# Feed-forward weight loads in twelve spaced parts, and an attention output matrix that is zeroed by VectorE and loaded early

## The chip, the cores and the metric

The kernel runs on one core of a Trainium2 chip (trn2). Its time is the device time of one launch in microseconds (us), the slowest core counting; here there is only one. Each execution also records the mean clock granted to TensorE (1.000 is full speed). "Fast" is an execution that is not over 1.5% above the fastest of the same kernel; only fast runs are compared. The engines are PE (TensorE, matrix products), PEld (its weight loads), DVE (VectorE), ACT (ScalarE), POOL (GpSimd) and SP (SyncE, which only issues DMA transfers here).

## The reference, cut to what matters

A transformer block: 2,048 tokens of width 512, 32 heads of width 16, a gated feed-forward layer of width 1,792, and a layer norm before each half whose shift, scale and gate come from a small conditioning vector.

```python
mod = (_silu(c) @ w_mod)            # sa, ca, ga, sb, cb, gb
h = _layernorm(x) * (1 + ca) + sa
q, k, v = split(h @ wqkv)           # 32 heads of 16
p = softmax(q @ k.T * 16 ** -0.5)
x = x + ga * ((p @ v) @ wo)
h = _layernorm(x) * (1 + cb) + sb
x = x + gb * (gelu(h @ w_gate) * (h @ w_up) @ w_down)
```

The costly part is the softmax: 32 x 2,048 x 2,048 exponentials.

## The kernel before: what the change touches

While it is built, the kernel plans its own instruction order. A recorder keeps a cost model of every engine; a loop (`stream`) places score products, exponentials and probability-times-value products, and slips side work (projections, output projection, feed-forward layer) into free TensorE time. What it decides is then fixed: each engine executes its list in order and waits on semaphores. So any change to the recorded operations can also change the order of everything after it.

Most exponentials are ScalarE instructions (`E<-ps_sc`) of three or two 512-column banks. About one bank in thirteen (156 of 2,048) is computed by VectorE in five steps (`dt`, `du`, `du`, `dt`, `ED`) to relieve ScalarE.

The step that finishes the conditioning vector (`modB`) frees the space in which the feed-forward weights are to lie. Everything that waited for that was put right behind it:

```python
    def side_mod(self):
        ...
        self.copy("dve", self.modB[:, :], mi[:, 0:8])
        self.ts("dve", self.modB[:, 4:8], self.modB[:, 4:8], 1.0, None, ALU.add)
        sp, pool = "sp", "pool"
        self.memset(pool, self.wo[:, :, :], 0.0, [self.modB[:, :]])     # after modB
        self.memset(pool, self.self32[:, :], 0.0)
        ...
        self.dma(sp, self.wg[:, :, :], ..., "wg")       # 1,792 KB each
        self.dma(sp, self.wu[:, :, :], ..., "wu")
        self.dma(sp, self.wd[:, :, :], ..., "wd")
        for j in range(4):
            for ee in range(2):                          # 8 loads of 64 KB
                src = self.A_wo.rearrange(...)[j, ee]
                self.dma(sp, self.wo[32 * j:32 * j + DH, ee:8:2, :], src, "wo%d" % (2 * j + ee))
```

`wo` is stored with 16 of every 32 partitions zero, hence the memset.

The same SyncE list carries the small transfers of the softmax denominators. After the last product of a group of four heads, VectorE copies the sums out (`osb`), and four kinds of transfers follow: `scr_den<-osb`, `den<-scr_den`, then after a reciprocal `scr_rec<-rden` and `rb<-scr_rec`. VectorE then forms `onorm = osb * rb`, at a fixed place in its list:

```python
        def fin1():
            self.recip(rden, den)
            self.dma("sp", s2..., rden, "dc%d" % sem)                    # scr_rec<-rden
            for j in range(4):
                self.dma("sp", self.rb[32 * j:32 * j + 32, lo:hi], ...)  # rb<-scr_rec
        def fin2():
            self.tt("dve", self.onorm[:, qd, c:c + W], osb, rb, ALU.mult)
```

The softmax here doesn't subtract the row's maximum and nothing guards it: scores larger than these inputs give would overflow.

## Time and profile before

| | before |
|---|---|
| time, median of three runs | 927.5 us (926.55 to 1,074.73; the longest is slow) |
| span of the profiled run | 925.9 us, clock 0.994 |
| ScalarE busy | 891.0 us, 96% |
| TensorE, VectorE busy | 809.4 us, 767.7 us |
| ScalarE idle from 79 to 125 us | 46.00 - 41.30 = 4.70 us |

The page's span, its busy line, and its chain of waits that ended last (shares of the span, by engine):

```profile
span 925.9 us, 17469 instructions
...
PE 809.4 (87%) x7328; PEld 259.3 (28%) x7328; DVE 767.7 (83%) x1483; ACT 891.0 (96%) x749; POOL 7.7 (1%) x13
...
ACT 82%; PE 8%; DVE 6%; DMA 3%; issue 1%; SPq 0%; DVEq 0%
```

ScalarE is the engine to read. The table by stretches shows where it is not full. Columns: the stretch in us, its length, then for each engine the busy time and the number of instructions, the granted TensorE clock, the DMA share and GB/s.

```profile
core 0: us, PE busy (x) PEld busy (x) DVE busy (x) ACT busy (x) POOL busy (x), PEclk, DMA share, GB/s
46.00:79.00 33.00, 30.48 (x264) 11.35 (x261) 15.93 (x28) 33.00 (x31) 0.00 (x0) 1.00 0.01 2
79.00:125.00 46.00, 38.45 (x315) 12.06 (x312) 39.95 (x67) 41.30 (x34) 4.41 (x3) 0.93 0.51 151
...
231.00:400.00 169.00, 147.39 (x1029) 38.50 (x1025) 154.22 (x285) 168.25 (x140) 0.00 (x0) 1.00 0.05 11
400.00:600.00 200.00, 173.00 (x1227) 46.11 (x1224) 180.48 (x332) 198.87 (x165) 0.00 (x0) 1.00 0.05 14
```

From 79 to 125 us ScalarE is busy 41.30 of 46 us, and the clock averages 0.93. The timeline of ScalarE in the stretch shows the gaps (start, time from there, instruction, count, and in brackets the idle time before it and what ended it):

```profile
88.52 7.52 ACT L309 ACTIVATE E<-ps_sc 128x1536 bf16<-128x1536 f32 x6 [1.35 <-PE ps_sc L296]
96.27 16.29 ACT L309 ACTIVATE E<-ps_sc 128x1536 bf16<-128x1536 f32 x13 [0.22 <-PE ps_sc L296]
113.80 2.54 ACT L309 ACTIVATE E<-ps_sc 128x1024 bf16<-128x1024 f32 x2 [1.25 <-PE ps_sc L296]
116.94 2.96 ACT L309 ACTIVATE E<-ps_sc 128x1536 bf16<-128x1536 f32 x2 [0.60 <-PE ps_sc L296]
120.48 3.77 ACT L309 ACTIVATE E<-ps_sc 128x1024 bf16<-128x1024 f32 x3 [0.58 <-PE ps_sc L296]
124.71 10.91 ACT L309 ACTIVATE E<-ps_sc 128x1024 bf16<-128x1024 f32 x9 [0.46 <-PE ps_sc L296]
```

What runs on Pool when the hole begins, from its timeline:

```profile
81.76 3.51 POOL L337 MEMSET wo<- 128x4096 bf16 x1 [77.46 <-DVE modB L321]
```

And what VectorE's `dt<-dt` takes beside it and just after, from VectorE's timeline:

```profile
81.77 3.77 DVE L321 TENSOR_SCALAR dt<-dt 128x512 f32<-128x512 int32 x1
...
88.56 0.41 DVE L321 TENSOR_SCALAR dt<-dt 128x512 f32<-128x512 int32 x1
```

The second is the same instruction at its usual length, 0.41 against 3.77 us. And SyncE's list, from its timeline, where the time is that spent issuing:

```profile
83.82 0.42 SPq L359 DMA_DIRECT2D mreg<-in_B_w_gate_dram  x1
84.29 0.51 SPq L359 DMA_DIRECT2D mreg<-in_B_w_up_dram  x1
84.84 0.51 SPq L359 DMA_DIRECT2D dreg<-in_B_w_down_dram  x1
85.39 12.25 SPq L359 DMA_DIRECT2D wo<-in_A_wo_dram  x8
97.68 0.42 SPq L359 DMA_DIRECT2D scr_rec<-rden  x1
105.74 1.71 SPq L359 DMA_DIRECT2D rb<-scr_rec  x4
```

The eight `wo` issues hold SyncE for 12.25 us. The view of the tile `wo` gives the shortest, the median and the longest issue in ns:

```profile
L359 SPq DMA_DIRECT2D wo<-in_A_wo_dram x8: 426/426/8970, 85.4 to 97.2; - x8
```

So the first one, right behind the three weight loads, is held for 8.97 us, and each of the other seven takes 0.43 us. In the chain of waits, between 70 and 130 us, the next small transfer follows:

```profile
97.68 8.04 DMA scr_rec<-rden
...
109.14 0.69 DVE onorm L313
```

It takes 8.04 us, and VectorE can form `onorm` only at 109.14 us, after 1.5 us of waiting. What VectorE has in its list behind `onorm` is late with it: TensorE waits 2.11 us until VectorE has made `kmo` (keys for the score products), ScalarE 1.25 us for scores. The record of the clock in this trace shows TensorE at half rate for 6.83 us from 113.5 us on, right behind TensorE's wait, and the gaps of 0.60 and 0.58 us lie in that.

### The profile page before, as it was taken

Reading aid. Unit: us, or ns where it says so; the run is one execution under the profiler, and the core shown is the slowest. Engines: PE = TensorE matmul, PEld = TensorE weight load, DVE = VectorE, ACT = ScalarE, POOL = GpSimd, SP = SyncE. Lnnn points to the kernel's source line nnn. Section 1 sums busy time; section 2 is a strip of 40 time slices with the busy share of each in tenths; the row PEclk is TensorE's granted clock in tenths of the full one; section 3 lists DMA queues with packets and bytes.
Section 4 is the critical chain, followed back from the end, with each engine's and each line's share of the span. In section 5 each row is a group of like instructions: output and inputs, shape, how many; then the busy total and the mean of one; then the engine's idle time right before and its main releaser. Section 6 shows DMA issues by size and latency. Waiting matters only on the chain.

```text
span 925.9 us, 17469 instructions
## 1 busy us (share of the span) xinstructions
PE 809.4 (87%) x7328; PEld 259.3 (28%) x7328; DVE 767.7 (83%) x1483; ACT 891.0 (96%) x749; POOL 7.7 (1%) x13
## 2 busy tenths in 40 slices
PE   8898888878889888888888888888898899988988
PEld 3332222222222222222222222222222223334346
DVE  8748889998997999998897999998998674577864
ACT  6999999999999999999999999999999999999992
POOL 1001000000000000000000000000000000000000
PEclk9999999999999999999999999999999999999999
DMA  9003500000000000000000000000010000000000
GB/s 296 1 1 135 154 13 12 13 13 13 14 13 7 8 12 14 13 13 20 13 18 12 14 13 13 13 1 19 25 26 9 13 8 19 25 14 13 21 8 13
DMA packets 30784, 24.96 MB, mean 27 GB/s; under 512 B 15705, under 2 KB 25490, under 8 KB 30706
## 3 DMA queue, kind: packets, MB, share of 16 engines
q1 hardware_dynamic: 28322, 22.28, 8.5%
q10 hardware_dynamic: 2384, 1.57, 0.6%
q8 instruction: 57, 0.93, 0.4%
q14 instruction: 21, 0.17, 0.1%
HBM read 21.23 MB, written 2.61 MB: 26 GB/s over the span
## 4 chain that ended last, share of the span: by engine, by line
ACT 82%; PE 8%; DVE 6%; DMA 3%; issue 1%; SPq 0%; DVEq 0%
ACT E L309 79%; PE ps_mi L296 4%; PE ps_sc L296 3%; ACT wreg L309 2%; DMA scr_rec<-rden 1%; DVE dt L321 1%; DMA mreg<-in_w_mod_dram 1%; DMA rb<-scr_rec 1%; PE ps_pv L296 1%; DVE du L326 1%; DVE wreg L326 1%; DVE ED L326 1%; DVE wreg L330 1%; SPq L359 0%; DVE onorm L313 0%
## 5 line engine op out<-in xcount | busy, mean ns | idle before, releaser
L309 ACT ACTIVATE E<-ps_sc 128x1536 bf16<-128x1536 f32 (+2 forms) x700 | 864.4, 1467 | 18.2 <-PE ps_sc L296 17.9
L296 PE MATMUL ps_pv<-E,vaug 128*17 128x512 bf16 (+2 forms) x2439 | 184.1, 330 | 3.6 <-ACT E L309 1.4
L296 PE MATMUL ps_sc<-qT,kme 32*128 32x512 bf16 (+2 forms) x1344 | 155.0, 331 | 26.0 <-ACT E L309 20.7
L296 PE MATMUL ps_sc<-qT,kmo 32*128 32x512 bf16 (+2 forms) x1344 | 156.4, 333 | 22.1 <-ACT E L309 17.3
L321 DVE TENSOR_SCALAR dt<-ps_sc 128x512 int32<-128x512 f32 x156 | 107.6, 690 | 41.8 <-PE ps_sc L296 37.8
L296 PE MATMUL ps_mi<-wreg,mreg 128*128 128x512 bf16 (+1 forms) x448 | 122.8, 358 | 12.2 <-DVE wreg L330 5.9
L296 PE MATMUL ps_sc<-xs,ident 128*128 128x512 bf16 x283 | 92.7, 386 | 35.8 <-ACT E L309 32.9
L326 DVE SCALAR_TENSOR_TENSOR ED<-du,dt 128x512 int16<-128x512 f32 x156 | 106.3, 684 | 0.7
L326 DVE SCALAR_TENSOR_TENSOR du<-du,dt 128x512 f32<-128x512 f32 x156 | 105.4, 681 | 0.5
L326 DVE SCALAR_TENSOR_TENSOR du<-dt 128x512 f32<-128x512 uint16 x156 | 105.3, 684 | 0.3
L296 PEld LDWEIGHTS ps_sc<-qT,kme 32*128 32x128 bf16 x1344 | 41.0, 91 | 140.6 <-ACT E L309 92.6
L296 PEld LDWEIGHTS ps_sc<-qT,kmo 32*128 32x128 bf16 x1344 | 41.5, 91 | 135.3 <-ACT E L309 90.8
L296 PEld LDWEIGHTS ps_pv<-E,vaug 128*17 128x17 bf16 x2439 | 48.1, 88 | 105.8 <-issue 94.4
L321 DVE TENSOR_SCALAR dt<-dt 128x512 f32<-128x512 int32 x156 | 67.8, 439 | 0.6
L296 PE MATMUL ps_mi<-dreg,hreg 128*128 128x512 bf16 x210 | 65.1, 385 | 0.5 <-DVE xw L313 0.2
L296 PE MATMUL ps_pv<-ED,vaug 128*17 128x512 bf16 (+2 forms) x185 | 59.2, 351 | 1.2 <-DVE ED L326 1.2
L296 PEld LDWEIGHTS ps_mi<-wreg,mreg 128*128 128x128 bf16 x448 | 34.9, 97 | 76.8 <-issue 37.1
L330 DVE CAST wreg<-ps_mi 128x512 bf16<-128x512 f32 x49 | 33.7, 688 | 22.9 <-PE ps_mi L296 22.4
L296 PEld LDWEIGHTS ps_sc<-xs,ident 128*128 128x128 bf16 x283 | 20.1, 97 | 85.9 <-ACT E L309 82.8
L296 PE MATMUL ps_mi<-hreg,wreg 128*128 128x512 bf16 x120 | 40.0, 390 | 1.9 <-DVE qT L321 1.1
L326 DVE SCALAR_TENSOR_TENSOR wreg<-wreg,ps_mi 128x512 bf16<-128x512 bf16 x49 | 33.5, 684 | 8.3 <-PE ps_mi L296 7.5
L296 PE MATMUL ps_mi<-wo,onorm 128*128 128x512 bf16 x120 | 38.2, 385 | 1.4 <-DVE xw L313 1.3
(118 smaller groups left out, 510.1 us busy)
## 6 DMA issues: line engine op xcount, KB each, us to landing
rb<-scr_rec SPq DMA_DIRECT2D x96, 64.0 KB, 2.0
mreg<-in_w_mod_dram SPq DMA_DIRECT2D x1, 2048.0 KB, 14.4
out_dram<-xs SPq DMA_DIRECT2D x16, 128.0 KB, 1.7
mreg<-in_B_w_gate_dram SPq DMA_DIRECT2D x1, 1792.0 KB, 7.1
mreg<-in_B_w_up_dram SPq DMA_DIRECT2D x1, 1792.0 KB, 11.2
dreg<-in_B_w_down_dram SPq DMA_DIRECT2D x1, 1792.0 KB, 16.5
rb<-scr_rec SPq DMA_DIRECT2D x56, 32.0 KB, 1.8
wreg<-in_A_wqkv_dram SPq DMA_DIRECT2D x3, 384.0 KB, 10.6
```

Source lines behind the costliest of these rows:

```text
L296: return self.rec("pe", lambda e: e.matmul(out, lhsT, rhs, start=start, stop=stop, tile_position=tp), [lhsT, rhs], [out], cost=(n, int(rhs ...
L309: return self.rec("act", lambda e: e.activation(out, in_, func, scale=scale, **kw), rd, wr, cost=self.cost("act", out, [in_], "act"))
L321: return self.rec(eng, lambda e: e.tensor_scalar(out, a, s1, s2, **kw), rd, [out], cost=self.cost(eng, out, [a], "ts"))
L326: return self.rec("dve", lambda e: e.scalar_tensor_tensor(out, a, s, b, op0=op0, op1=op1), rd, [out], cost=self.cost("dve", out, [a, b], " ...
L330: return self.rec(eng, lambda e: e.tensor_copy(out, in_), [in_], [out], cost=self.cost(eng, out, [in_], "ts"))
```

## The change

The intent: no burst of 5.4 MB ahead of the small transfers, and no long Pool memset while VectorE computes exponentials. The zeros of `wo` become eight VectorE memsets, done with the `wo` loads some 30 us earlier. The feed-forward weights are loaded in twelve parts, eight score banks apart.

```diff
     def side_mod(self):
         ...
-        self.memset(pool, self.wo[:, :, :], 0.0, [self.modB[:, :]])
-        self.memset(pool, self.self32[:, :], 0.0)
+        self.done("modB")
+        yield END
+
+    def side_wo_load(self):
+        if not self.dry:
+            self.task([lambda qd=qd: self.memset("dve", self.wo[:, qd, :], 0.0) for qd in range(8)]
+                      + [lambda: self.memset("dve", self.self32[:, :], 0.0)], "wo0")
+        yield from self.until("wo0")
         ...                                  # affine_select on Pool, as before
-        self.dma(sp, self.wg[:, :, :], ..., "wg")        # and wu, wd: whole
         ...                                  # the eight wo loads, as before
+
+    def weight_parts(self):                  # 4 of wg, 4 of wu, 4 of wd
+        ...
     def plan(self, ends, nsplit):
         w = [(self.side_first, 0, at(30))]
+        w.append((self.side_wo_load, at(30), at(30)))
     def stream(self):
+        parts = self.weight_parts()
         while rp < len(rounds):
+            while parts and "modB" in self.have and pos >= loaded:
+                parts.pop(0)()
+                loaded = pos + 8
```

More of the change, by code (lines that the diff above doesn't have):

```diff
@@ L765, in side_mod @@
         self.ts("dve", self.modB[:, 4:8], self.modB[:, 4:8], 1.0, None, ALU.add)
-        sp, pool = "sp", "pool"
-        self.memset(pool, self.wo[:, :, :], 0.0, [self.modB[:, :]])
-        self.memset(pool, self.self32[:, :], 0.0)
+        self.done("modB")
[5 more added lines that the diff above has]
+        yield from self.until("wo0")
         selv = self.self32[:, :].rearrange("p (a b) -> p a b", b=32)
         self.affine_select(selv, [[-32, 4], [0, 32]], ALU.not_equal, 1.0, -16, 1)
-        self.dma(sp, self.wg[:, :, :], self.B_w_gate.rearrange("(a p) n -> p a n", p=P), "wg")
-        self.dma(sp, self.wu[:, :, :], self.B_w_up.rearrange("(a p) n -> p a n", p=P), "wu")
-        self.dma(sp, self.wd[:, :, :], self.B_w_down.rearrange("(f p) n -> p f n", p=P), "wd")
         for j in range(4):
@@ L776, in side_mod, with part @@
                 src = self.A_wo.rearrange("(a j e r) n -> j e r a n", j=4, e=2, r=DH)[j, ee]
-                self.dma(sp, self.wo[32 * j:32 * j + DH, ee:8:2, :], src, "wo%d" % (2 * j + ee))
+                self.dma("sp", self.wo[32 * j:32 * j + DH, ee:8:2, :], src, "wo%d" % (2 * j + ee))
         yield END
+    def weight_parts(self):
+        def part(dst, src, sem):
+            return lambda: self.dma("sp", dst, src, sem)
+        parts = []
+        for name, t, w in (("wg", self.wg, self.B_w_gate), ("wu", self.wu, self.B_w_up)):
+            v = w.rearrange("(a p) n -> p a n", p=P)
+            parts += [part(t[:, a, :], v[:, a, :], "%s%d" % (name, a)) for a in range(NDC)]
+        v = self.B_w_down.rearrange("(f p) n -> p f n", p=P)
+        parts += [part(self.wd[:, f:f + 4, :], v[:, f:f + 4, :], "wd%d" % f) for f in range(0, 12, 4)]
+        parts.append(part(self.wd[:, 12:NFC, :], v[:, 12:NFC, :], "wd12"))
+        return parts
     def ln2_steps(self, k, src=None):
@@ L1055, in stream @@
         active = []
-        pos = c = e = nd = rp = 0
+        pos = c = e = nd = rp = loaded = 0
         virt = 0.0
```

## The prediction

> **What bounds it.** ScalarE: busy 891.0 of 925.9 us (96%) on the page, and the chain that ended last runs 79% over its Exp instructions. So from 20 to 900 us time is saved only where ScalarE stands idle, or by giving it fewer columns. The stage table shows it full from 23 to 79 us, losing time between 79 and 125 us, full again to about 845 us; its other idle time lies in the first 20 us and the tail, which the diff leaves alone.
>
> **The hole at 79 to 125 us.** ScalarE's timeline has six gaps there: 1.35, 0.22, 1.25, 0.60, 0.58, 0.46 us, together 4.46 us. Two causes, both edited by the diff:
> 1. Pool's memset of wo runs at 81.76 for 3.51 us. Meanwhile one VectorE TENSOR_SCALAR dt<-dt takes 3.77 us (usually 0.42): 3.35 us of VectorE lost. The Trainium skill ("SBUF — State Buffer", "Who interferes with whom") says a VectorE two-port mode and GpSimd exclude each other for a whole instruction; this trace agrees. The 1.35 us gap follows.
> 2. Three 1,792 KB loads and eight wo loads are issued at 83.8 to 97.6 us, the wo issues alone holding SyncE for 12.25 us (1.5 us each; rb issues take 0.43). The next scr_rec gets out only at 97.68 and lands 8.04 us later (chain); rb lands at 109.0. VectorE waits 1.50 us for it in order, TensorE then 2.11 us for kmo, ScalarE 1.25 us. TensorE's thin stretch at 110 to 113 halves its granted clock (0.50 from 114 to 120 us), which makes the gaps of 0.60 and 0.58. "TensorE: Matmul & The Clock Gate" (Part 1) describes that gate; its half rate agrees.
>
> **The change.** Removed: the Pool memset and the burst of 5.4 MB. Added on VectorE: eight 128x256-word memsets, 0.27 us each by the equal-sized dreg memset at 0.92 us, and a small one: about 2.4 us, in the 46 to 69 us stretch where VectorE is busy 9.3 of 23 us: free. It delays side projections by 2.4 us; ScalarE is full there, so they have slack. wo loads start near 50 us on an empty queue. Each of twelve parts is 448 KB (last: 256): at the trace's 350 to 430 GB/s an estimated 1.1 to 1.3 us, some 3 us apart, so a small transfer waits about 1 us instead of 8.
>
> The built order also differs: 154 VectorE exponentials for 156, hence two Exp of 1,536 columns more and two of 1,024 fewer, at ScalarE spacings of 1.34 and 0.91 us: +0.9 us. The two are lost near the onset of VectorE exponentials, about 80 us.
>
> **Sum.** 927.5 - 4.5 (perhaps 0.5 stays) + 0.9 = about 924. Later stages are reshuffled but equally ScalarE-bound: within 1 us or so. VectorE time won back buys nothing more, as the recorded order is fixed.
>
> **What will show it.** On Pool one 0.5 us select near 50 us in place of the burst; no dt<-dt above 0.5 us near 82; scr_rec landing in 2 to 4 us; no half-clock stretch at 113 to 120; ScalarE idle below 1 us from 79 to 125; ScalarE busy 1 us up.
>
> **What would make it wrong.** A new half-clock stretch elsewhere, or the later onset of VectorE exponentials; then no gain. If the rest runs denser than I think, 920 or less. Beyond 2% either way is out of reach: the idle time there is 4.5 us.
>
> Predicted 924.0 us, range 921.0 to 927.3; faster by over 2% 0.01, within 2% 0.98, slower 0.01.

## The result, and the profile after

The changed kernel takes 922.4 us (median of four fast runs, 921.53 to 923.05) against 927.02 us (four runs, with the slow one). The ratio of the fast runs is 0.9956, with a 95% interval of 0.9936 to 0.9976. Ratios here and below are the mean time of one kernel's fast runs over that of the other's of the same rounds, so not quite the ratio of the medians quoted. That is 0.4%. Another chip gave 0.9961 (e7 below).

The page's span, busy line and chain:

```profile
span 919.5 us, 17368 instructions
...
PE 779.0 (85%) x7222; PEld 259.7 (28%) x7342; DVE 759.8 (83%) x1482; ACT 890.8 (97%) x749; POOL 3.6 (0%) x11
...
ACT 89%; PE 6%; DVE 3%; issue 0%; DMA 0%; DVEq 0%
```

(PE's line isn't compared: the page after lists 120 fewer products than weight loads, the page before none.) The table by stretches, columns as before:

```profile
46.00:79.00 33.00, 29.31 (x256) 11.55 (x260) 16.75 (x35) 32.83 (x30) 0.31 (x1) 1.00 0.11 26
79.00:125.00 46.00, 38.84 (x364) 13.35 (x363) 41.97 (x75) 46.00 (x40) 0.00 (x0) 1.00 0.40 133
...
231.00:400.00 169.00, 142.05 (x1015) 38.20 (x1030) 151.51 (x279) 168.77 (x140) 0.00 (x0) 1.00 0.04 11
400.00:600.00 200.00, 168.33 (x1208) 45.85 (x1227) 180.05 (x334) 199.34 (x165) 0.00 (x0) 1.00 0.05 15
```

ScalarE is full from 79 to 125 us, the clock is 1.00 there, and the two losses between 231 and 600 us have shrunk from 0.75 + 1.13 to 0.23 + 0.66 us. ScalarE's timeline from 70 to 140 us has one gap left:

```profile
76.95 64.53 ACT L309 ACTIVATE E<-ps_sc 128x1536 bf16<-128x1536 f32 x53 [0.17 <-PE ps_sc L296]
```

On Pool one short operation is left after 5 us, by its timeline:

```profile
54.15 0.31 POOL L340 TENSOR_SCALAR_AFFINE_SELECT self<-self 128x128 f32<-128x128 f32 x1 [49.86 <-DVE self L337]
```

`dt<-dt` has its usual length, two of them in 0.76 us, by VectorE's timeline:

```profile
84.44 0.76 DVE L321 TENSOR_SCALAR dt<-dt 128x512 f32<-128x512 int32 x2
```

SyncE's list, from its timeline:

```profile
53.62 3.62 SPq L359 DMA_DIRECT2D wo<-in_A_wo_dram  x8
...
80.97 0.35 SPq L359 DMA_DIRECT2D mreg<-in_B_w_gate_dram  x1
83.41 0.33 SPq L359 DMA_DIRECT2D scr_rec<-rden  x1
84.82 1.72 SPq L359 DMA_DIRECT2D rb<-scr_rec  x4
86.58 1.37 SPq L359 DMA_DIRECT2D mreg<-in_B_w_gate_dram  x3
88.00 0.94 SPq L359 DMA_DIRECT2D mreg<-in_B_w_up_dram  x2
```

The `wo` loads take 3.62 us to issue into an empty queue. `scr_rec` is issued at 83.41 and lands 1.4 us later, as the first `rb` goes out at 84.82. But the parts are not evenly spaced on the chip: parts two to six leave together, within 2.4 us from 86.58 us on, since SyncE works in order and had waited for `scr_rec` to land. From 92 to 94 us the DMA still moves 384 GB/s.

The profiled pair differs by more than the medians, 925.9 - 919.5 = 6.4 us. Part of that is luck: the profile before has a second stretch at half clock, near 900 us, which the profile after has not. Such stretches come and go between runs (see "What the Trainium skill lacked").

### The profile page after: what moved, and what is told of

It reads as the page before. It is cut to its first block, busy times and chain, and to the rows that moved or that the text cites. A ratio compares the mean times of both kernels' runs of the same rounds, so it can differ in the third digit from the quotient of the medians.

```text
span 919.5 us, 17368 instructions
## 1 busy us (share of the span) xinstructions
PE 779.0 (85%) x7222; PEld 259.7 (28%) x7342; DVE 759.8 (83%) x1482; ACT 890.8 (97%) x749; POOL 3.6 (0%) x11
## 4 chain that ended last, share of the span: by engine, by line
ACT 89%; PE 6%; DVE 3%; issue 0%; DMA 0%; DVEq 0%
ACT E L309 87%; PE ps_sc L296 3%; PE ps_mi L296 2%; ACT wreg L309 2%; PE ps_pv L296 1%; DVE du L326 0%; DVE st L349 0%; DMA xs<-in_A_x_dram 0%; DVE xw L313 0%; DVE nwt L313 0%; DVE dt L321 0%; ACT hreg L309 0%; DVE hreg L321 0%; DVE wreg L326 0%; ACT L309 0%
## 5 line engine op out<-in xcount | busy, mean ns | idle before, releaser
L309 ACT ACTIVATE E<-ps_sc 128x1536 bf16<-128x1536 f32 (+2 forms) x700 | 865.2, 1489 | 12.9 <-PE ps_sc L296 12.9
L296 PE MATMUL ps_pv<-E,vaug 128*17 128x512 bf16 (+2 forms) x2439 | 180.1, 329 | 3.3 <-DVE vaug L330 1.1
L296 PE MATMUL ps_sc<-qT,kmo 32*128 32x512 bf16 (+2 forms) x1344 | 154.1, 331 | 31.1 <-ACT E L309 26.4
L296 PE MATMUL ps_sc<-xs,ident 128*128 128x512 bf16 x264 | 85.7, 384 | 47.0 <-ACT E L309 45.1
L296 PE MATMUL ps_mi<-wreg,mreg 128*128 128x512 bf16 (+1 forms) x421 | 113.9, 355 | 11.8 <-DVE wreg L326 4.5
L321 DVE TENSOR_SCALAR dt<-dt 128x512 f32<-128x512 int32 x154 | 63.8, 417 | 0.5
L296 PE MATMUL ps_mi<-dreg,hreg 128*128 128x512 bf16 x185 | 56.5, 384 | 2.4 <-issue 1.3
L296 PE MATMUL ps_mi<-hreg,wreg 128*128 128x512 bf16 x105 | 34.0, 385 | 2.5 <-DVE qT L321 0.9
L313 DVE TENSOR_TENSOR wreg<-wreg 128x1024 bf16<-128x1024 bf16 (+1 forms) x56 | 34.7, 619 | 0.5
```

The source lines that it names most:

```text
L296: return self.rec("pe", lambda e: e.matmul(out, lhsT, rhs, start=start, stop=stop, tile_position=tp), [lhsT, rhs], [out], cost=(n, int(rhs ...
L309: return self.rec("act", lambda e: e.activation(out, in_, func, scale=scale, **kw), rd, wr, cost=self.cost("act", out, [in_], "act"))
L313: return self.rec(eng, lambda e: e.tensor_tensor(out, a, b, op), [a, b], [out], cost=self.cost(eng, out, [a, b], "tt"))
L321: return self.rec(eng, lambda e: e.tensor_scalar(out, a, s1, s2, **kw), rd, [out], cost=self.cost(eng, out, [a], "ts"))
```

## The experiments

Comparing the two kernels alone can't tell the causes apart, since the planner gave them different orders. So most experiments keep the order of the kernel before. The recorder got a mode in which an operation is recorded, with its waits, but not seen by the cost model, and a "ghost" that enters the cost of an operation which is not there. The rivals A to D are other explanations; each is stated in the expectation of the run that tests it. Checked instruction by instruction: TensorE's and ScalarE's lists in e1 to e5 and e8 are those of the kernel before, and VectorE's differ by the nine memsets alone.

```diff
     def model(self, op, t, cost):
+        if self.quiet:
+            op.t1 = 0.0
+            return
+    def ghost(self, eng, t, cost, dma=False):
+        ...
+        op = _Op(eng, "d_ghost" if dma else eng, 0, None)
+        self.model(op, max(t, self.free[eng]), cost)
+        return op.t1
```

All experiments compute the right result. Each has five rounds beside the kernel before, on one chip per call (e1 to e4, e5 to e8, e9 to e12); medians are of fast runs. As TensorE, ScalarE and VectorE do the same work in the same order, the time from the 51st to the 101st exponential instruction of ScalarE in the trace measures the hole by itself. It is in the last column, for one profiled execution of each. (Line numbers in the profiles of the experiments are shifted by the added code: L325 is the ScalarE helper that was L309.)

| run | zeros | wo loads | weights | median, us (before) | ratio, 95% interval | 51st to 101st Exp, us |
|---|---|---|---|---|---|---|
| before | Pool, 82 us | after weights | whole | | | 65.56 |
| e1 | VectorE, early | after weights | whole | 928.62 (927.95) | 1.0017 (0.9999 to 1.0036) | 65.64 |
| e2 | Pool, 82 us | before weights | parts | 924.57 (927.95) | 0.9967 (0.9951 to 0.9984) | |
| e3 | VectorE, early, and a Pool memset at 82 us | early | parts | 924.51 (927.95) | 0.9982 (0.9955 to 1.0008) | 61.37 |
| e4 | VectorE, early | early | parts | 924.09 (927.95) | 0.9970 (0.9949 to 0.9991) | 61.03 |
| e5 | VectorE, early | early | whole | 923.35 (927.18) | 0.9959 (0.9944 to 0.9974) | 59.89 |
| e8 | Pool, early | early | parts | 923.57 (927.18) | 0.9974 (0.9951 to 0.9997) | 59.89 |

### e1: only the zeros moved

```diff
-        self.memset(pool, self.wo[:, :, :], 0.0, [self.modB[:, :]])
+        wz = self.ghost(pool, at, 8 * D * 3.0 + 100)     # the plan still sees it
+    def zero(self):                                      # recorded quietly at at(30)
+        for qd in range(8):
+            self.memset("dve", self.wo[:, qd, :], 0.0)
```

> Every instruction of TensorE, ScalarE and VectorE is issued in the order of the kernel before; only the zeros of wo move, from one Pool memset after modB to eight VectorE memsets near 50 us. The three whole weight loads and the eight wo loads stay where they were. Theory (two separate causes, the exclusion of VectorE by the Pool memset worth the gaps of 1.35 and 0.22 us): 1.2 to 1.8 us faster than before, no dt<-dt above 0.5 us near 82 us, scr_rec still landing after about 8 us and the half-clock stretch near 113 us still there. Rival A (absorption: VectorE waits 1.5 us for rb later in any case, so the delay costs nothing in the end): within 0.5 us of before. Rival B (the whole gain is the new instruction order that the planner made): no gain.

No gain at all, where I expected 1.2 to 1.8 us. The long `dt<-dt` and the gap at 87 us are gone, but one gap takes the place of the others. ScalarE's timeline:

```profile
116.36 2.54 ACT L325 ACTIVATE E<-ps_sc 128x1024 bf16<-128x1024 f32 x2 [4.78 <-PE ps_sc L312]
```

SyncE's timeline:

```profile
86.29 12.52 SPq L375 DMA_DIRECT2D wo<-in_A_wo_dram  x8
98.85 0.42 SPq L375 DMA_DIRECT2D scr_rec<-rden  x1
107.75 1.71 SPq L375 DMA_DIRECT2D rb<-scr_rec  x4
```

VectorE, freed earlier, reaches `onorm` earlier and waits there: 4.5 us at one time in the list of waits of that stretch, against 1.5 us before. `scr_rec` still takes 8.9 us. The end of the hole is set by the transfer, so the 3.35 us that VectorE lost to the Pool memset were hidden in front of it. Rival A holds here; the theory of two separate costs falls.

### e2: only the loads in parts

```diff
-        self.dma(sp, self.wg[:, :, :], ..., "wg")        # and wu, wd
+        self.ghost(sp, t, P * 3584 * 4, True)            # one for each; parts quietly in stream
```

> Instruction order of the kernel before on all compute engines; the three loads are issued as twelve spaced parts; the Pool memset of wo and the eight wo loads stay after modB. Theory: the second cause goes and the first stays: scr_rec lands in under 4 us, rb before 95 us instead of 109, no half-clock stretch near 113 us, ScalarE's gaps between 100 and 125 us gone and the 1.35 us gap at 87 us kept: 2.5 to 3.3 us faster than before. Rival B (order): no gain. Rival C (it is the wo loads, waiting on the memset and holding SyncE, and not the size of the burst): gap near 110 us stays, gain under 1 us.

The gain is 3.4 us by the medians, about as expected. `scr_rec` lands in 3.5 us (issued at 90.54, the first `rb` at 94.06). The eight `wo` loads, still at the old place but with an empty queue in front of them, are issued in 3.62 us instead of 12.25. What remains of the hole (0.67, 0.51 and 0.22 us) is partly a half-clock stretch at 83 us that this run happened to have. Its last column is left out for that.

### e3 and e4: all but the exclusion, and all

```diff
 # e3 is e4 with this in the place of the old memset:
+        self.quietly(lambda: self.memset(pool, self.onorm[:, 1:8, :], 0.0, [self.modB[:, :]]))
```

> Instruction order of the kernel before; zeros and wo loads early, loads in twelve parts, and a Pool memset of 128x3584 elements of onorm that nobody needs is put where the memset of wo was. Only the exclusion of VectorE is left of the two causes: the memset takes about 3.1 us, one VectorE dt<-dt takes about 3.3 us near 82 us. Theory: 1.0 to 1.6 us slower than e4_all_order_kept, with a ScalarE gap of about 1 us at 87 us. Rival A (absorbed): as fast as e4_all_order_kept within 0.5 us.

> All three parts of the change, but every instruction of TensorE, ScalarE and VectorE in the order of the kernel before (156 VectorE exponentials instead of 154). Theory: ScalarE idle between 79 and 125 us under 0.5 us, no half-clock stretch near 113 us, 4 to 5.5 us faster than before, and up to 1 us faster than the changed kernel, which gives ScalarE 0.9 us more of columns. Rival B (the gain comes from the new order): within 1 us of before. If it is slower than the changed kernel by over 1 us, the planner's new order is worth something of its own.

The medians, 924.51 and 924.09 us, do not separate the two; both scatter with the clock (0.985 to 1.000). The traces do. In e3 the useless memset runs at 82.64 us for 3.08 us, and the instruction beside it, from VectorE's timeline, is

```profile
82.65 3.35 DVE L337 TENSOR_SCALAR dt<-dt 128x512 f32<-128x512 int32 x1
```

ScalarE's timeline of e3:

```profile
88.88 7.52 ACT L325 ACTIVATE E<-ps_sc 128x1536 bf16<-128x1536 f32 x6 [0.83 <-PE ps_sc L312]
96.62 55.04 ACT L325 ACTIVATE E<-ps_sc 128x1536 bf16<-128x1536 f32 x45 [0.22 <-PE ps_sc L312]
```

The gain of e4 over before, 3.9 us by the medians, is just under the 4 us expected, and rival B (order) falls, since e4 has the old order. In e3 the two gaps of the first cause are there, 0.83 and 0.22 us, where e5 and e8 have none. By the last column the exclusion costs 61.37 - 59.89 = 1.48 us once the transfer is out of the way. The two runs of e3 at clock 0.999 and 1.000 have a span of 921.7 us each, the one of e4 at 1.000 has 920.6: 1.1 us. (The profiled run of e4 had a half-clock stretch of 3.41 us at 83 us, hence its 61.03.) So the predicted price of the memset, 1.35 + 0.22 us, was about right, but it is paid only after the other cause is gone.

### e5 and e6: whole loads again, the rest of the change kept

e5 has the order before, e6 the planner's own.

```diff
 # e5: wo and its zeros early; wg, wu, wd as in the kernel before
 # e6, on the changed kernel:
-        parts += [...]                                   # twelve parts
+        parts = [lambda: (self.dma("sp", self.wg[:, :, :], ...), self.dma("sp", self.wu[:, :, :], ...),
+                          self.dma("sp", self.wd[:, :, :], ...))]
```

> Order of the kernel before; zeros by VectorE and wo loads near 55 us, but the three weight loads whole and together after modB. Nothing holds SyncE now, so scr_rec is issued near 86 us instead of 98, behind 5.4 MB in the same queue. Theory (the queue is served in order, so what counts is how many bytes stand ahead): at the 350 to 430 GB/s of the earlier traces the burst drains near 100 us, scr_rec takes 12 to 15 us to land, rb lands near 103 us instead of 109; ScalarE keeps a gap of 0 to 2 us near 105 to 110 us; 2.5 to 4.5 us faster than before. Rival C (the hold of SyncE by the eight wo issues was the whole delay): scr_rec lands in under 4 us. Rival D (splitting matters as much as moving wo): rb still later than 107 us and under 1.5 us gained.

> The changed kernel with only the twelve parts undone: the three loads whole, at the place of the first part. The planner makes its own order from its own DMA model. Theory: scr_rec behind the burst, 10 us or more to land; 0.5 to 2.5 us slower than the changed kernel of this call. If it is equal within 0.5 us, the parts are not needed once wo is early and its zeros are off Pool.

> The changed kernel on this chip, as the control. Expected 4 to 6 us faster than before. Theory: at equal granted clock 0 to 1.2 us faster than e4_all_order_kept was (best of that 920.6 us of span at clock 1.000), because its own order leaves about 1 us less of ScalarE gaps between 231 and 600 us, which pays for the 0.9 us of extra columns.

e6 takes 922.34 us (ratio 0.9953, 0.9937 to 0.9970) and e7, the changed kernel on the same chip, 923.5 us (0.9961, 0.9947 to 0.9975). The twelve parts are not needed. (e7's gain over before is 3.7 us by the medians, just under the 4 to 6 expected.) SyncE's timeline of e5:

```profile
84.28 0.42 SPq L375 DMA_DIRECT2D mreg<-in_B_w_gate_dram  x1
84.75 0.51 SPq L375 DMA_DIRECT2D mreg<-in_B_w_up_dram  x1
85.30 0.51 SPq L375 DMA_DIRECT2D dreg<-in_B_w_down_dram  x1
85.85 8.97 SPq L375 DMA_DIRECT2D scr_rec<-rden  x1
102.54 1.72 SPq L375 DMA_DIRECT2D rb<-scr_rec  x4
```

ScalarE's timeline of e5:

```profile
69.77 81.77 ACT L325 ACTIVATE E<-ps_sc 128x1024 bf16<-128x1024 f32 x68
```

`scr_rec` is held for 8.97 us in its issue alone and lands 16.7 us after it began: longer than before. Yet ScalarE has no gap. What counts is when it lands: 102.5 us. In e1, which differs from e5 only in the place of the `wo` loads, and whose weights left 0.45 us later, it lands at 107.7 us. So the eight `wo` loads between the weight loads and it delay it by 107.7 - 102.5 - 0.45 = about 4.7 us. The traffic shows them. From the table by stretches, two microseconds of e1:

```profile
102.00:104.00 2.00, 2.00 (x24) 0.95 (x22) 1.50 (x4) 2.00 (x3) 0.00 (x0) 1.00 1.18 114
```

The same stretch of e5:

```profile
102.00:104.00 2.00, 2.00 (x25) 0.98 (x24) 1.50 (x3) 2.00 (x3) 0.00 (x0) 1.00 0.10 36
```

The last two columns are the DMA share and GB/s. In e1 the DMA engines are busy throughout and move 114 GB/s, where the big loads (98 to 100 us) moved 354. `wo` is loaded in 64 KB pieces whose rows are 1 KB. In e5 the queue is nearly empty by then. The margin is thin: in e5 VectorE waits 0.3 us for `rb`, in the kernel before 1.5 us.

So rivals C and D both fall. The hold of SyncE is there in e5 too and costs nothing: it strikes the first transfer issued behind the three whole loads, whichever that is (`wo` before, 8.97 us, and in e1, 9.23 us; `scr_rec` in e5, 8.97 us). And the split adds nothing. My own expectation for e6, 0.5 to 2.5 us slower than the change, was a miss as well.

The Trainium skill says in "DMA: Bandwidth & Descriptors", "Queues, rings and completion order", that on each DMA engine descriptors are consumed in ring order. The 16.7 us behind the burst in e5, against 1.4 us in the changed kernel, agree.

### e8: the zeros on Pool, early

```diff
+        self.memset("pool", self.wo[:, :, :], 0.0, [self.vaug[:, 12, 0:1]])   # near 50 us
```

> Order of the kernel before, parts, wo early, and the zeros by the old Pool memset, but near 50 us instead of 82. Theory (it is the time of the memset and not the engine that counted): as fast as e4_all_order_kept or 0.3 to 0.6 us faster, because the 2.4 us of VectorE memsets near 51 us, behind which e3 and e4 show 0.4 us of ScalarE idle before 79 us, are gone; VectorE may stall once for up to 3.5 us near 51 us. Rival (Pool memsets hurt wherever they stand): 1 us or more slower than e4.

The Pool memset runs from 51.95 us for 3.51 us, and nothing is lost: ScalarE is full from 23 to 200 us, and the small gaps near 56 and 61 us that e3 to e5 have behind the VectorE memsets are gone (33.00 of 33 us busy from 46 to 79 us, against 32.59). The only VectorE instruction inside the memset reads PSUM, the memory that the matrix products are written to, and takes its usual 0.69 us. That agrees with the Trainium skill: "SBUF — State Buffer", "Who interferes with whom", says that a VectorE instruction with at most one SBUF input, outside the two-port modes, does not contend with Pool. By the median e8 equals e5 (one of its six runs, at clock 0.987, pulls its ratio up). It is the time of the memset that hurt, not its engine.

### e9 to e12: looking for a better version

Half-clock stretches remain in all versions. The planner issues filler products to keep TensorE busy; `FILL` is its target of columns.

```diff
-FILL = 4200
+FILL = 4800        # e9, e10; 5400 in e12
 # e10 and e11: the changed kernel with its zeros on Pool, near 50 us
```

> The changed kernel with the planner's fill target for TensorE raised from 4200 to 4800 columns per 3,413 ns, which puts 493 filler matmuls in place of 321 and, because the planner finds less room, 152 VectorE exponentials in place of 154. Theory (the half-clock stretches of 3.41 us that turn up at different places in nearly every run are set off by thin TensorE stretches, and each costs about 0.7 us): mean clock 0.999 or 1.000 in most runs, spread of the runs under 1.5 us, 0.9 us lost on two more ScalarE banks: median 0 to 1.5 us faster than the changed kernel. Rival (stretches are not set by the kernel's fill): clocks spread from 0.992 to 0.999 as before and about 1 us slower.

> As e9, with the zeros of wo made by one Pool memset near 50 us, off VectorE's list: 155 VectorE exponentials. Theory: 0.4 to 1.2 us faster than e9, the fastest of this call if the fill helps, 920.5 to 922 us median.

> The changed kernel with only the zeros of wo put back on Pool, but near 50 us. Planner's own order with 154 VectorE exponentials. Theory (the time of the memset counts and not its engine): equal to the changed kernel within 1 us, ScalarE gap near 77 us gone.

> As e9 with a target of 5400: 710 fillers and 149 VectorE exponentials, five more banks on ScalarE, 2.1 us. Theory: clock 1.000 in all runs but the extra ScalarE columns cost more than is saved: 0 to 2 us slower than e9. Rival: slower by more, because fillers get in the way of the score matmuls (more and longer ScalarE gaps).

| run | median, us (before 926.3) | ratio, 95% interval | clocks of its runs |
|---|---|---|---|
| e9 | 924.57 | 0.9979 (0.9968 to 0.9991) | 0.998 to 1.000 |
| e10 | 922.35 | 0.9954 (0.9940 to 0.9967) | 0.994 to 1.000 |
| e11 | 924.52 | 0.9972 (0.9955 to 0.9989) | 0.991 to 0.998 |
| e12 | 928.43 | 1.0019 (1.0004 to 1.0035) | 0.995 to 1.000 |

In e9 four of five runs have a clock of 0.999 or 1.000, as expected. But e10 and e12, with the same target or a larger one, fall to 0.994 and 0.995, so it isn't shown that more filler holds the clock up. e9 was expected to be up to 1.5 us faster than the change and looks slower (0.9979 against 0.9956 and 0.9961, intervals overlapping; on other chips, at clock 0.999 or 1.000, spans of 922.3 to 922.5 us against 919.5 to 919.9). Its plan has 152 VectorE exponentials, hence two more banks on ScalarE, and another order. e12, expected at most 2 us slower than e9, is 3.9 us slower by the medians, and 2.3 to 3.4 us at clock 1.000 (spans of 924.8 to 925.7 us against 922.3 to 922.5). e10 is level with the change (0.9954 against 0.9956 and 0.9961, all intervals overlapping), and just above the 920.5 to 922 us expected of it, so no version here clearly beats it. e9 and e10 differ by 2.2 us although both have the larger target: e9 has three more banks on ScalarE, an estimated 1.3 us at the prediction's 0.9 us for two, and the rest isn't explained. e11, expected to equal the change within 1 us, can't be told from it: the change was not in that call, and e11's clocks were low. Its gap near 77 us is gone, as expected.

## Why the prediction was right, point by point

- **The time.** Predicted 924.0 us (921.0 to 927.3), measured 922.4. Right, and right for the main reason: ScalarE's hole from 79 to 125 us closes completely (41.30 to 46.00 of 46 us busy).
- **Size of the hole.** Mis-sized. The prediction put down its idle time, 4.46 us (six gaps; all of it is 4.70 us). With the same instructions in the same order, e5 and e8 need 59.89 us for the fifty exponentials that took 65.56: 5.67 us. Idle time is not all that a gap costs. An Exp after a gap lasts 1.45 us, while back to back they start 1.34 us apart. The overlap lost, 0.11 us at each of nine gaps (the six and three under 0.12 us), is an estimated 1.0 us, which is about the difference. These are single profiles, and not all of the 5.67 us reaches the end: by the medians e5 and e8 gain 3.8 and 3.6 us.
- **"Two causes", added up.** The step that failed in its form. The exclusion of VectorE by Pool is real (e3), and its price is the predicted one (1.48 us, against 1.35 + 0.22), but in the kernel before it was covered by the wait for the transfer: e1 gains nothing. Alone, the second cause is worth the most of it (e2, 3.4 us).
- **"The burst of 5.4 MB".** Named too broadly. The three weight loads alone do not make the small transfer late enough to cost anything (e5), and the eight `wo` loads alone do not either (e2); the `wo` loads behind the weight loads do (e1 against e5, 4.7 us). Either cure is enough: `wo` early (e5), or parts with `wo` in front (e2). Nor is a `wo` issue slow, as the prediction's "1.5 us each" has it: that is the mean of one held for 8.97 us by the weight loads and seven of 0.43 us. That a small transfer must not wait 8 us, as the prediction had it, was wrong: it waits 16.7 us in e5 at no cost.
- **Half clock at 114 to 120 us.** It goes with the hole: it is in the profiles of before and e1 (which have the hole) at 114 and 112 us, and in no other profile at that place. "TensorE: Matmul & The Clock Gate" (Part 1) has the clock halved after an idle window of about 3.4 us. The lengths agree: the stretches here are 3.41 or 6.83 us. The idleness does not: in the 3.41 us before this stretch TensorE was busy for 1.30 us, so a thin stretch came before the halving and not an idle one. Here the measurement decides.
- **Parts "some 3 us apart".** Wrong: five of them left within 2.4 us, since SyncE works in order. It did no harm, as e5 explains.
- **VectorE memsets free.** Nearly: 2.19 us for eight, as costed, and a ScalarE gap of 0.17 us near 77 us, which is not there in e11.
- **"+0.9 us" of columns, and "ScalarE busy 1 us up".** Two more instructions of 1,536 columns and two fewer of 1,024 are there, but busy time fell by 0.2 us (891.0 to 890.8). The likely reason, not tested alone: the ends of instructions that gaps expose count as busy, and there are fewer gaps. The planner's order also lost 0.23 + 0.66 us between 231 and 600 us instead of 0.75 + 1.13, which pays for the columns. e8, e5 and e4 have the old order and keep the two old gaps there. The prediction had allowed "within 1 us or so" for this.

What stays open: why the planner's order saves those two gaps, and how much of the 0.5 to 1.2 us by which e6 and the change (spans of 919.3 to 919.9 us at clock 0.999 or 1.000, on two chips) lead e5 (920.4 and 920.5) is due to them; and why thin stretches of TensorE halve the clock in one run and not in another.

## What to carry to other kernels

When several causes delay the same engine, look at which wait ends last before adding their prices: removing the one that is covered gains nothing until the other is gone, and each must then be tested with the other absent. A transfer's landing time against its deadline matters, not its latency: find what stands in front of it in the queue, and move enough of that into an idle time. A merged line of a timeline can hide one long instruction among short ones, so look at the longest before calling all of them slow. In a kernel that plans its own order, hold the order fixed to learn what a change itself is worth; otherwise 1 or 2 us of new order hide it.

## What the Trainium skill lacked or had wrong

- "TensorE: Matmul & The Clock Gate" (Part 1) speaks of idle windows that halve the clock. Here the 3.41 us before a stretch at half clock were thin and not idle: TensorE was busy for 1.30 us of them before the stretch at 113 us (kernel before), 2.24 us before the one at 238 us (e7) and 2.63 us before the one at 83 us (e4). The page gives no case of a kernel whose TensorE is about 85% busy. The stretches come at places that differ between profiles (83 us in e2 and e4, 203 us in e5 and e8, 238 us in e7, 329 us in e11), each 3.41 us long. Within one kernel, runs differ accordingly: in each of e1 to e12 a straight line through the runs gives 0.3 to 0.7 us for each 0.001 of mean clock, so an estimated 0.6 to 1.3 us for one stretch (3.41 x 0.5 / 921 = 0.0019). That is most of the scatter here.
- "SBUF — State Buffer" ("Who interferes with whom") is right about the exclusion: VectorE's 0.41 us instruction took 3.77 and 3.35 us beside Pool memsets of 3.51 and 3.08 us.
- "DMA: Bandwidth & Descriptors" gives no price for a small transfer behind a large one in the same queue, nor for large loads that hold the issuer: here 16.7 us to land behind 5.4 MB, with 8.97 us of that in the issue. The next transfer issued behind the three whole loads was held for 8.9 to 9.2 us in each of the four profiles that were looked at (before, e1, e5, e6), against 0.43 us for an issue otherwise.
